# A fused forgetting-attention and gated-FFN kernel: the written issue order and the engines of casts and copies are replaced

## The chip, the cores and the metric

The kernel runs on one core of one Trainium2 chip. The core has five engines with instruction streams of their own: TensorE (PE, matmuls and transposes), VectorE (DVE), ScalarE (ACT), GpSimd (POOL) and SyncE (SP, which here only issues DMA transfers). Each engine works through its own stream in order; semaphores tie the streams together. The metric is the device time of one execution in microseconds (us), as the median of several runs.

## The reference

Two layers are computed. The first is causal attention with a decay, for 8 batches of 8 heads, 576 positions and a head size of 64. The second is a feed-forward layer on its result, 512 to 1024 to 512 wide, with a gate that is a sigmoid of a three-tap convolution along the positions.

```python
scores = scale * np.matmul(q, k.transpose(0, 1, 3, 2))
cum = np.cumsum(np.log(np.clip(f, 0.0001, 1.0)), axis=-1)
scores = np.where(causal, -1e9, scores + cum[:, :, :, None] - cum[:, :, None, :])
attn = softmax(scores)
x = np.matmul(attn, v)                 # (8, 8, 576, 64) -> (8, 576, 512)
h = np.maximum(x @ w_in, 0.0)          # (8, 576, 1024)
conv = conv_w[0] * h[s - 1] + conv_w[1] * h[s] + conv_w[2] * h[s + 1]
out = (h * sigmoid(conv)) @ w_out      # (8, 576, 512)
```

## The kernel before, in words

The work is cut into 16 half-batches (hb) of four heads each for attention, and 8 batches (b) for the feed-forward layer. All of it is written as named tasks. `add` registers a task with its engine, the tasks it comes after, and the buffers it takes and gives back. `Plan.play` then walks through one long list, ORDER, and issues each task in turn. ORDER therefore sets the order of the instructions on every engine and of the transfers on SyncE's queue, and also which of the rotating buffers a task gets. A task name with `@ACT`, `@DVE`, `@POOL` or `@SP` names its engine too, where the task can run on more than one.

The names, for half-batch hb, pair of heads i = 2 hb or 2 hb + 1, batch b, and chunk ff of 128 hidden units:

- Loads on SP: `q{hb}.0` and `q{hb}.1` load the queries and keys of a half-batch by a transposing DMA (line 178); `v{b}.{kb}` loads a block of values of a batch (L207); `wi{j}` and `wo{j}` load quarters of the weights (L496). `rw{hb}` (L200, L201), and from half-batch 8 on `fi{hb}` (L192, L194), put the rows with the decay sums beside the queries and keys; no score of that half-batch can start before them. `s{b}.{a}` stores outputs, `tx14` and `tx15` turn the last attention results by DMA (L416).
- Attention: `cl` clears the odd or even rows of the loaded queries or keys on DVE (L184); for half-batches 0 and 1 it brings in tiles that PE turned (`tp`, L164). `sd`, `so`, `st` are the score matmuls of the diagonal blocks, of the others, and of the tail of 64 positions (L310, with a mask by L318 in half-batches 0 to 7). `ed`, `eo`, `et` are their exponentials on ACT (L351, L368, L330). `md`, `mt` mask on POOL from half-batch 8 on (L354, L333). `va{hb}.0` and `va{hb}.1` cast the values to 16 bits (L215 large, L217 small). `pv` multiplies with the values (L387, L392), `n` divides by the sums (L400, L401), `t` turns the result on PE (L410) and `tx` copies it out of PSUM (L413).
- Feed-forward: `f` first product (L425), `r` relu on ACT (L435), `c` and `d` the two steps of the convolution on DVE (L440, L442), `a` the tanh that makes the sigmoid (L445), `g` the gate on DVE (L449), `o` second product (L456, L460), `e` evacuation of the result (L466, L471). `wic`, `woc` cast the weights (L504).

PSUM is held as four tiles of 128 x 1024, and every PE task but the continuation of a chunk needs a free one. The queries and keys have a ring of four tiles, so the loads of half-batch hb wait for the scores of hb - 4. The values as loaded have two tiles, the cast values four.

SP issues the transfers strictly in their written order, and each engine waits at the head of its stream. So a task that waits holds all that stands behind it on its engine, and a load stands behind all loads written before it.

## Time and profile before

| | us |
|---|---|
| three runs | 249.54, 249.56, 249.83 |
| median | 249.56 |
| profiled execution, from its first to its last instruction (span) | 248.9 |
| median minus span | 0.66 |
| busy in the span: PE, DVE, ACT, POOL | 232.9, 215.9, 211.1, 46.0 |
| granted clock of PE, mean | 0.998 |

Of the profiled execution only the span is told; its time with what lies around it was not noted apart from the runs. The views used below are: the page with the busy time of each engine; the same by stretches of the span; the timeline of an engine, with the start, the length, the line, the operation and what is written from what is read; the groups by line and form, with the busy time of a group, the mean length of one instruction in ns, the idle time before them and what ended it; the waits; and the chain of waits, followed back from the last instruction. A matmul's length in a row holds its pipeline too, so the step from one start to the next is the better price of a matmul.

### The profile page before, as it was taken

To read this page: it belongs to the slowest core of one execution; us is meant where nothing else is said; L and a number is where in the kernel's file an instruction comes from. 1 tells how busy PE (TensorE), PEld (TensorE's weight loads), DVE (VectorE), ACT (ScalarE), POOL (GpSimd) and SP (SyncE) were. 2 spreads that over 40 slices of the span, in tenths; PEclk is the share of its full clock that TensorE was granted. 3 is DMA by queue.
4 is the path that set the end of the run, shared out by engine and by line. 5 is a ranking of instruction groups with operands and counts; after the bars stand their busy time and mean duration, and the time that the engine had idled before them with its cause. 6 is when DMAs were issued, how large, how long until landed. Compare 5 with 4: busy or idle time off the path is not lost.

```text
span 248.9 us, 6646 instructions
## 1 busy us (share of the span) xinstructions
PE 232.9 (94%) x2750; PEld 151.3 (61%) x2750; DVE 215.9 (87%) x328; ACT 211.1 (85%) x286; POOL 46.0 (18%) x76
## 2 busy tenths in 40 slices
PE   0899999879899999999999999999999999999993
PEld 0787785557556856666556765577557756645441
DVE  5654278999999999999999999997999999999961
ACT  2766958999999999979999899998999999767642
POOL 8000411101021501002203070045012502000000
PEclk9999999999999999999999999999999999999999
DMA  7987999999998999999999999899960590223345
GB/s 199 297 157 171 253 226 238 178 276 180 264 201 155 261 173 237 244 250 250 211 271 275 230 188 266 235 230 154 244 188 3 145 320 7 50 47 108 121 153 191
DMA packets 117062, 48.81 MB, mean 196 GB/s; under 512 B 106402, under 2 KB 107618, under 8 KB 117032
## 3 DMA queue, kind: packets, MB, share of 16 engines
q1 hardware_dynamic: 116578, 47.51, 85.3%
q0 software_dynamic: 208, 0.51, 0.7%
q8 instruction: 21, 0.34, 0.6%
q10 hardware_dynamic: 246, 0.37, 0.5%
q14 instruction: 9, 0.07, 0.1%
HBM read 21.11 MB, written 10.17 MB: 126 GB/s over the span
## 4 chain that ended last, share of the span: by engine, by line
PE 68%; DVE 12%; ACT 9%; DMA 6%; issue 3%; ACTq 0%; SPq 0%; DVEq 0%
PE ps L456 18%; PE ps L425 18%; PE ps L310 13%; PE ps L387 6%; PE ps L460 3%; DVE u L440 3%; DMA qk<-in_q_dram 3%; DVE u L442 3%; PE ps L318 2%; DMA u<-in_f_dram 2%; PE ps L410 2%; ACT pp L368 2%; PE ps L392 2%; ACT hg L445 2%; DVE hg L449 2%
## 5 line engine op out<-in xcount | busy, mean ns | idle before, releaser
L425 PE MATMUL ps<-xt,w_in_f 128*128 128x512 f16 (+1 forms) x512 | 68.4, 286 | 1.6 <-DMA xt<-xm 0.6
L368 ACT ACTIVATE pp<-ps 128x1024 f16<-128x1024 f32 x64 | 65.4, 1043 | 4.9 <-PE ps L310 2.6
L310 PE MATMUL ps<-qk 128*128 128x128 bf16 (+2 forms) x576 | 64.4, 241 | 1.8 <-DVE xm L401 0.6
L456 PE MATMUL ps<-w_out_f,hg 128*128 128x512 f16 x256 | 59.2, 379 | 0.0
L442 DVE SCALAR_TENSOR_TENSOR u<-ht,cwt,u 128x576 f32<-128x576 f16 x64 | 53.8, 854 | 1.4
L440 DVE SCALAR_TENSOR_TENSOR u<-ht,cwt 128x576 f32<-128x576 f16 x64 | 53.1, 837 | 2.3 <-ACT ht L435 2.2
L445 ACT ACTIVATE hg<-u,cw 128x576 f16<-128x576 f32 x64 | 48.9, 784 | 5.7 <-DVE u L442 5.7
L425 PEld LDWEIGHTS <-w_in_f 128*128 128x128 f16 x512 | 34.0, 98 | 31.0 <-issue 2.5
L310 PEld LDWEIGHTS <-qk 128*128 128x128 bf16 x576 | 39.6, 98 | 18.9 <-issue 3.8
L449 DVE SCALAR_TENSOR_TENSOR hg<-hg,ht 128x576 f16<-128x576 f16 x64 | 49.8, 800 | 1.0 <-ACT hg L445 0.9
L435 ACT ACTIVATE ht<-ps 128x576 f16<-128x576 f32 x64 | 41.3, 669 | 3.3 <-PE ps L425 3.2
L456 PEld LDWEIGHTS <-hg 128*128 128x128 f16 x256 | 24.0, 98 | 25.9 <-issue 0.2
L354 POOL TENSOR_SCALAR_AFFINE_SELECT pp<-pd 128x1024 f16<-128x1024 f32 x16 | 18.6, 1171 | 48.2 <-ACT pd L351 42.4
L387 PE MATMUL ps<-va,pp 128*128 128x65 f16 x640 | 24.6, 193 | 0.7 <-ACT pp L368 0.5
L401 DVE TENSOR_TENSOR xm<-ps,rc 128x896 f16<-128x896 f32 (+1 forms) x32 | 24.3, 758 | 1.1
L387 PEld LDWEIGHTS <-pp 128*128 128x128 f16 x640 | 22.4, 97 | 3.0 <-ACT pp L368 1.0
L351 ACT ACTIVATE pp<-ps 128x1024 f16<-128x1024 f32 x16 | 16.5, 1038 | 4.7 <-PE ps L315 2.4
L466 ACT COPY ob<-ps 128x1024 f32<-128x1024 f32 (+1 forms) x18 | 15.1, 838 | 3.4 <-PE ps L456 2.5
L351 ACT ACTIVATE pd<-ps 128x1024 f32<-128x1024 f32 x16 | 15.9, 1022 | 1.9 <-PE ps L310 1.9
L318 PE MATMUL ps<-mask,ident 128*128 128x512 bf16 (+1 forms) x40 | 14.8, 369 | 0.3 <-ACT xt L413 0.2
L184 DVE TENSOR_SCALAR qk<-qk,lim 128x2304 uint16<-128x2304 uint16 x12 | 11.2, 933 | 1.1 <-DMA qk<-in_k_dram 0.9
L333 POOL TENSOR_SCALAR_AFFINE_SELECT pt<-p 128x256 f16<-128x256 f32 x8 | 4.8, 596 | 38.6 <-ACT p L330 36.9
(86 smaller groups left out, 193.2 us busy)
## 6 DMA issues: line engine op xcount, KB each, us to landing
vf<-in_v_dram SPq DMA_DIRECT2D x32, 256.0 KB, 4.8
out_dram<-ob SPq DMA_DIRECT2D x14, 512.0 KB, 4.9
qk<-blank SPq DMA_DIRECT2D x8, 540.0 KB, 5.9
ob<-in_moe_w_in_dram SPq DMA_DIRECT2D x4, 512.0 KB, 4.8
ob<-in_moe_w_out_dram SPq DMA_DIRECT2D x4, 512.0 KB, 4.9
vf<-in_v_dram SPq DMA_DIRECT2D x8, 128.0 KB, 5.2
out_dram<-ob SPq DMA_DIRECT2D x4, 256.0 KB, 2.1
out_dram<-ob SPq DMA_DIRECT2D x15, 64.0 KB, 3.2
```

What stands on the lines that cost most here:

```text
L310: nc.tensor.matmul(o, tk[:, h * S + k0:h * S + k0 + 128], tq[:, h * S + q0:h * S + q0 + n], start=first, stop=last and not by_matmul(hb, h))
L351: nc.scalar.activation(o, ps_of(f"sd{i}").rearrange("p (s c) -> p s c", s=2), AF.Exp, scale=SCALE)
L368: nc.scalar.activation(pair(i)[:, s, 512:1536], ps_of(f"so{i}.{s}"), AF.Exp, scale=SCALE)
L387: nc.tensor.matmul(ps[:, c:c + D + 1], block(hb, h, m, n), va[:, h, m, 0:D + 1], start=(m == 0), stop=(m == n))
L401: nc.vector.tensor_tensor(xm[:, CUT * D * u:CUT * D * u + nj * k * D].rearrange("p (j x d) -> p j x d", x=k, d=D), got[:, :, :, 0:D], r.un ...
L425: nc.tensor.matmul(ps[:, t0:t1], w_in_f16[:, cc, 128 * ff:128 * (ff + 1)], xt[:, cc // 2, x:x + t1 - t0], start=(cc == 0), stop=(cc == NCC ...
L435: nc.scalar.activation(ht_of(b, ff)[:, 1:1 + S], ps_of(f"f{b}.{ff}")[:, 0:S], AF.Relu, scale=0.5)
L440: nc.vector.scalar_tensor_tensor(u, ht[:, 0:S], cwt[:, ff, 0:1], ht[:, 1:1 + S], op0=ALU.mult, op1=ALU.add)
L442: nc.vector.scalar_tensor_tensor(u, ht[:, 2:2 + S], cwt[:, ff, 1:2], u, op0=ALU.mult, op1=ALU.add)
L445: nc.scalar.activation(hg_of(b, ff), u_t[slot[f"c{b}.{ff}", "u"]], AF.Tanh, scale=cw[:, ff, 1:2])
L449: nc.vector.scalar_tensor_tensor(hv, hv, 1.0, ht_of(b, ff)[:, 1:1 + S], op0=ALU.add, op1=ALU.mult)
L456: nc.tensor.matmul(ps[:, 512 * (c % 2):512 * (c % 2 + 1)], hg_of(b, ff)[:, 128 * c:128 * (c + 1)], w_out_f16[:, ff, :], **kw)
```

## The change

Only the list ORDER is replaced. It holds the same tasks, each once, and their functions are unchanged; so are the buffers, matmuls and transfers. What moves is the order on all engines and on SP's queue, and the engine of some casts and copies:

| task (lines) | before | after |
|---|---|---|
| large value casts va.0 (L215) | 9 DVE, 3 ACT, 4 POOL | 6 DVE, 1 ACT, 9 POOL |
| small value casts va.1 (L217) | 4 DVE, 6 ACT, 6 POOL | 2 DVE, 6 ACT, 8 POOL |
| copies of turned tiles tx (L413) | 10 DVE, 4 ACT | 9 DVE, 5 ACT |
| large evacuations e (L466) | 1 DVE, 13 ACT | 3 DVE, 11 ACT |
| small evacuations e (L466) | 2 DVE, 5 ACT | 1 DVE, 6 ACT |
| evacuations of the last batch (L471) | 1 DVE, 4 ACT | 5 ACT |
| weight casts wic, woc (L504) | 3 ACT, 5 POOL | 2 ACT, 6 POOL |

The first words of the list, and those at its end from the last product with the values to the first product of batch 7:

```diff
-dca cw ld0 ld0.0.0 tp0.0.0 dcl ld0.1.0 ld0.0.1 tp0.0.1 tp0.1.0 v0.0 ld1 ld0.1.1 ld1.0.1 ld1.0.0 dcs dck q2.1 ki@SP
+ld1 ld0 ld0.0.0 ld0.1.0 ld0.0.1 v0.0 ld0.1.1 ld1.0.1 cw ld1.0.0 dca dcl tp0.0.0 q2.1 tp0.0.1 cl0.0.0@ACT dcs tp0.1.0
...
-pv15.1 r6.7 c6.6 a6.5 o5.2 n15.0 n15.1 tx14 tx15 c6.7 d6.7 a6.7 d6.6 o5.3 g6.3 g6.7 e5.1@ACT f7.0
+pv15.1 n15.0 c6.6 o5.0 r6.7 n15.1 c6.7 o5.1 d6.7 c6.4 s3.1 a6.7 s4.1 s4.2 tx14 g6.7 g6.2 d6.4 a6.3 tx15 r6.5 d6.6 o5.2 c6.5 f7.0
```

SP's queue from the rows of half-batch 6 (the first two rows) to those of half-batch 7 (the last two), before. L178 is a transposing load of queries or keys, L207 a load of values; qk0 to qk3 are the ring, so half-batch 7 is in qk3 and 8 and 9 are in qk0 and qk1:

```order
L200 DMA qk2_87<-image_65 1x2304
L201 DMA qk2_87<-image_65 2x2304
L178 DMA_TRANSPOSE qk3_88<-in_k_dram 128x2304
L207 DMA vf1_90<-in_v_dram 128x8x64
L207 DMA vf1_90<-in_v_dram 64x8x64
L207 DMA vf1_90<-in_v_dram 128x8x64
L178 DMA_TRANSPOSE qk1_86<-in_q_dram 128x2304
L200 DMA qk3_88<-image_65 1x2304
L201 DMA qk3_88<-image_65 2x2304
```

The same piece of SP's queue after the change:

```order
L200 DMA qk2_87<-image_65 1x2304
L201 DMA qk2_87<-image_65 2x2304
L207 DMA vf1_90<-in_v_dram 128x8x64
L178 DMA_TRANSPOSE qk1_86<-in_k_dram 128x2304
L178 DMA_TRANSPOSE qk3_88<-in_q_dram 128x2304
L178 DMA_TRANSPOSE qk1_86<-in_q_dram 128x2304
L207 DMA vf1_90<-in_v_dram 64x8x64
L207 DMA vf1_90<-in_v_dram 128x8x64
L207 DMA vf0_89<-in_v_dram 128x8x64
L200 DMA qk3_88<-image_65 1x2304
L201 DMA qk3_88<-image_65 2x2304
```

Both loads of half-batch 9 (qk1) and a first load of batch 4's values (vf0) now stand ahead of half-batch 7's rows; in the whole queue 52 of these tasks stood ahead of them before and 56 do now, the four more being q9.1, v3.2, v3.3 and v4.0.

POOL's casts ahead of its first masks, before (ob0 to ob2 hold loaded weights, vf0 and vf1 loaded values):

```order
L215 CAST va1_92<-vf0_89 128x4x4x64
L217 CAST va1_92<-vf0_89 64x4x64
L504 CAST w_in_f16_69<-ob0_127 128x2x512
L504 CAST w_in_f16_69<-ob2_129 128x2x512
L504 CAST w_in_f16_69<-ob1_128 128x2x512
L217 CAST va3_94<-vf1_90 64x4x64
L504 CAST w_out_f16_70<-ob2_129 128x1024 x2
```

And after the change:

```order
L504 CAST w_in_f16_69<-ob0_127 128x2x512
L504 CAST w_in_f16_69<-ob1_128 128x2x512
L215 CAST va0_91<-vf0_89 128x4x4x64
L215 CAST va3_94<-vf1_90 128x4x4x64
L504 CAST w_in_f16_69<-ob0_127 128x2x512
L504 CAST w_out_f16_70<-ob1_128 128x1024
L504 CAST w_out_f16_70<-ob0_127 128x1024
L504 CAST w_out_f16_70<-ob2_129 128x1024
L215 CAST va1_92<-vf0_89 128x4x4x64
```

The weights come first on POOL now, and large value casts stand between and behind them.

2 lines of the change are left out of this document (1 added, 1 removed).

## The prediction

> **What bounds the kernel now.** I read the page's busy shares first, then the same by stretches of 10 us, then the timelines of SyncE and TensorE at the places where loads arrive, the chain of waits, and groups by form.
>
> The page's first part:
>
> ```profile
> PE 232.9 (94%) x2750; PEld 151.3 (61%) x2750; DVE 215.9 (87%) x328; ACT 211.1 (85%) x286; POOL 46.0 (18%) x76
> ```
>
> TensorE (PE), VectorE (DVE) and ScalarE (ACT) are all near full over the span. The stretches tell where PE is not full (columns: busy us of PE, PEld, DVE, ACT, POOL with instruction counts, then granted PE clock, DMA share, GB/s):
>
> ```profile
> 40.00:50.00 10.00, 8.94 (x84) 5.25 (x82) 9.69 (x13) 9.76 (x15) 1.96 (x2) 1.00 1.18 198
> 50.00:60.00 10.00, 8.72 (x166) 6.66 (x166) 9.62 (x16) 9.97 (x13) 1.04 (x1) 1.00 1.08 249
> 60.00:70.00 10.00, 8.89 (x84) 5.39 (x82) 9.76 (x15) 10.00 (x14) 1.66 (x1) 1.00 1.05 210
> 70.00:80.00 10.00, 9.96 (x84) 5.42 (x82) 9.93 (x14) 9.82 (x15) 0.00 (x1) 1.00 0.96 196
> 80.00:90.00 10.00, 9.94 (x183) 7.71 (x180) 9.79 (x17) 9.43 (x13) 4.05 (x7) 1.00 1.10 222
> 140.00:150.00 10.00, 9.86 (x157) 7.39 (x154) 9.70 (x15) 9.15 (x14) 5.66 (x5) 1.00 1.12 211
> ```
>
> From 40 to 70 us PE idles 1.06 + 1.28 + 1.11 = 3.45 us, with ACT and DVE both full: those two bound it there. Behind 70 us PE is full and sets the pace. The DMA share is 0.96 to 1.18: the DMA engines are full as well. No instruction is added or removed, so a new order can win little more than those 3.45 us and what PE loses at the end (below). It can lose more than that.
>
> SyncE's timeline (start, length, line, transfer) decides how early attention inputs arrive, since one queue carries all loads in written order:
>
> ```profile
> 15.26 3.44 SPq L178 DMA_TRANSPOSE qk<-in_q_dram  x1
> 19.90 0.32 SPq L200 DMA_DIRECT2D qk<-image  x1
> ...
> 64.02 0.58 SPq L201 DMA_DIRECT2D qk<-image  x1
> ...
> 89.30 0.37 SPq L200 DMA_DIRECT2D qk<-image  x1
> 89.77 0.60 SPq L201 DMA_DIRECT2D qk<-image  x1
> ...
> 92.69 1.20 SPq L207 DMA_DIRECT2D vf<-in_v_dram  x2
> 93.93 3.27 SPq L178 DMA_TRANSPOSE qk<-in_k_dram  x1
> ```
>
> The queue issues nearly back to back; its one early pause is 18.70 to 19.90 us, 1.2 us, ahead of rw1. PE's timeline has the two places where half-batches 4 and 7 are first used:
>
> ```profile
> 66.77 0.38 PE L318 MATMUL ps<-mask,ident 128*128 128x512 bf16 x1
> ...
> 95.85 0.27 PE L318 MATMUL ps<-mask,ident 128*128 128x256 bf16 x1
> ...
> 96.17 1.06 PE L460 MATMUL ps<-w_out_f,hg 128*64 128x256 f16 x16
> ```
>
> The rows of half-batch 4 (rw4) finish issue at 64.60 and PE uses them at 66.77, so they land within 2.17 us. For half-batch 7 the rows finish issue at 90.37, could be used at 92.5, and are used at 95.85: 3.3 us to spare.
>
> **The change part by part.**
>
> *The start, to about 40 us: 0.* ACT, DVE and PE begin with the same tasks; PE's first difference is one score group moved ahead. The loads of w_in move forward on SyncE, ahead of rw1 and the v loads; the 1.2 us pause covers part of it. The first v load may then land up to 3 us later and hold PE by about 1 us, but at half-batch 7 that is absorbed by the wait below. Bounds −0.5 to +1, in the end 0.
>
> *40 to 95 us, compute: up to −2.8, covered by the next term.* I count, in the order, what ACT has to do between f0.3 and f1.7 (before) and between f0.3 and f1.5 (after); both stretches hold the same work of PE to within 0.3 us. After the change ACT has two relus, one tanh and four casts, copies or evacuations of 1024 columns less there; it has two score exponentials, two tail exponentials and two small v casts more. ACT's steps in the chain of waits:
>
> ```profile
> 79.03 1.23 ACT ht L435 x2
> 80.25 0.91 ACT pp L368
> 81.16 0.66 ACT hg L445
> ```
>
> That is 0.62 a relu, 0.91 an exponential, 0.66 a tanh; a copy of 1024 columns is 1.02 (row below), a small one a quarter of the columns, an estimated 0.3. So −1.24 − 0.66 − 4.1 + 1.8 + 1.2 = −3.0, of which I count 2.8 since some of the steps overlap. ACT is a full engine there, so 2.8 of the 3.45 us could come back.
>
> *Half-batch 7 on SyncE: +0.6.* Ahead of rw7 stand all the loads of before plus q9.1 and three v loads (v3.2, v3.3, v4.0). Their price by issue rows: the transpose at 93.93 is 3.3; two v loads take from 92.69 to 93.93, 0.62 each. That makes 5.2. By bytes, 0.59 MB (4 heads of 576 × 64 numbers of 4 bytes) and 3 × 0.26 MB (128 × 512 of them) at 215 GB/s, the mean of the stretches from 40 to 90 us, makes 6.4. I take 6.4, because the DMA engines are full. The pause of 1.2 us is filled now. So rw7 starts at 89.30 + 6.4 − 1.2 = 94.5, finishes 1.07 later, and lands by 97.7. PE reaches its first use (sd14) with st6 and o0.4 done besides. Tasks of their kind stand in the rows above: 95.85 to 96.17, 0.3 us, and the 1.06 us from 96.17, about 1.0 to the next. By the pace of before PE is there at 95.85 + 1.3 = 97.1. Difference +0.6; bounds: 5.2 − 1.2 gives −0.6, 6.4 without the pause gives +1.8. Whatever ACT's relief wins earlier is waited away at this one place, since sd14 stands ahead of everything else on PE.
>
> *From 98 us on: +0.3.* Before t8, t9 and f4.0 some cushions get short: only the nine transposes of t8 stand between pv9.1 and t9, where the second norm of half-batch 9 has to run in between. The nearest price is a short wait that PE has for such a step before (the view of waits: us in total, times, longest):
>
> ```profile
> PE ps L425 <- DVE xt L413: 0.3, 1, 0.3
> ```
>
> One such wait of 0.3 is taken; none, and one at each of the four tight steps (1.2), are the bounds.
>
> *The end: −0.6.* The last turned tiles come by DMA (tx14, tx15). PE's timeline there, before:
>
> ```profile
> 215.69 3.63 PE L456 MATMUL ps<-w_out_f,hg 128*128 128x512 f16 x16
> 219.15 0.65 PE L425 MATMUL ps<-xt,w_in_f 128*128 128x512 f16 x4
> 220.38 2.61 PE L425 MATMUL ps<-xt,w_in_f 128*128 128x512 f16 x20 [0.57 <-DMA xt<-xm]
> ```
>
> Between pv15.1 and f7.0 PE does two chunks of the output product (215.69 to 219.15, 1.73 each) and then waits 0.57 for tx15. After the change three chunks stand there, while DVE puts one more conv (0.81, row below) between the two norms: 1.73 − 0.81 covers 0.57. Bounds −0.6 to 0. Behind the last gate (g7.7) PE had fifteen matmuls of 512 columns and eight pairs of the last chunk to do; nine and seven pairs are left, so DVE may come in later than before by six matmuls before PE waits for it.
>
> *Casts and copies: 0, with a cost if the cover goes.* Rows by form (busy us, mean ns of one):
>
> ```profile
> L215 DVE CAST va<-vf 128x1024 f16<-128x1024 f32 x9 | 7.2, 797 | 5.2 <-DMA vf<-in_v_dram 5.2
> L215 POOL CAST va<-vf 128x1024 f16<-128x1024 f32 x4 | 4.6, 1161 | 33.5 <-DMA vf<-in_v_dram 33.5
> L466 ACT COPY ob<-ps 128x1024 f32<-128x1024 f32 x13 | 13.2, 1017 | 2.5 <-PE ps L456 2.5
> L413 DVE COPY xt<-ps 128x1152 f16<-128x1152 f16 x10 | 7.2, 751 | 1.0 <-PE ps L410 1.0
> ...
> L466 DVE COPY ob<-ps 128x1024 f32<-128x1024 f32 x1 | 1.2, 1217 | 0.0
> ```
>
> DVE gives up three large v casts (2.4 us), a turned copy (0.75) and four small ones (estimated at 0.4 each, half a large one), and takes two large evacuations (2.4): about −2.4 us. POOL takes five large casts (5.8), two small ones and a weight cast (estimated from these rows at 1.2 and 1.3): +8.3 us, on an engine that is 18% busy. But POOL slows DVE. The same DVE operations in a stretch with POOL idle (70 to 80 us) and one with POOL 5.66 us busy (140 to 150):
>
> ```profile
> L440 DVE SCALAR_TENSOR_TENSOR u<-ht,cwt 128x576 f32<-128x576 f16 x4 | 3.2, 810 | 0.0
> L449 DVE SCALAR_TENSOR_TENSOR hg<-hg,ht 128x576 f16<-128x576 f16 x4 | 3.0, 749 | 0.0
> ...
> L449 DVE SCALAR_TENSOR_TENSOR hg<-hg,ht 128x576 f16<-128x576 f16 x5 | 4.2, 879 | 0.0
> L440 DVE SCALAR_TENSOR_TENSOR u<-ht,cwt 128x576 f32<-128x576 f16 x1 | 1.6, 1644 | 0.0
> ```
>
> Excess 0.83 + 5 × 0.13 = 1.5 us for 5.66 of POOL, 0.26 each us. So 8.3 us more of POOL cost DVE 2.2, and its relief of 2.4 is spent. I take 0; bounds −0.5 and +2.2.
>
> [...]
>
> **The sum.** 0 + 0.6 + 0.3 − 0.6 + 0 = +0.3 on the span of 248.9. The median of the runs, 249.56, is 0.66 above the span, taken as unchanged: 249.8.
>
> **The rivals.** *Faster:* the v loads are as cheap as their issue rows and the DMA engines take more at once, so rw7 lands before PE comes and the relief of ACT stays. For it: the 3.45 us of PE idle and ACT's 2.8. Against it: DMA shares of 0.96 to 1.18. It gives between 249.56 − 0.6 − 0.6 = 248.4 (rw7 at its early bound) and 249.56 − 2.8 − 0.6 = 246.2 (no wait at all): 247.3. *Slower by POOL:* between the same f marks POOL had one small and two weight casts and gets three large and four weight casts, most of its 8.3 us, just where DVE is full at 9.62 to 9.76 of 10; if DVE's moved casts are of no use there, the price is 2.2 us. It decides once DVE's norms of half-batches 2 and 3 come later than the rows of half-batch 4, which PE waits for next: 249.8 + 2.2 = 252.0. On the same side, rw7 at its late bound (+1.8 for +0.6) gives 251.0.
>
> **How the numbers follow.** A kernel like this can be told from no change from about 0.2% on, 0.5 us. The wait at half-batch 7, as forecast: chance 0.50, own range 249.0 to 251.0, of which 0.27 lie within 0.2%, 0.20 above and 0.03 below. Faster: 0.25. POOL: 0.25, all slower. Faster 0.28, same 0.27, slower 0.45. The range leaves the outer half of the faster rival and little above POOL's: 247.2 to 252.2.
>
> **What would show it.** Right: rw7 issued at 93.3 to 95.7 us, PE waiting for it just behind, no wait on xt<-xm at the end. Wrong: PE waiting for DVE or POOL at 40 to 70 us, L440 and L449 above 900 ns there; rw7 before 92; or a stall of over 1 us past 100 us, of which no term speaks.

## The result, and the profile after

The new kernel takes 253.85 us (median; 252.69, 253.08, 254.62, 254.91), the kernel before 249.55 on the same chip (249.33 to 249.83). The ratio is 1.0157, 95% interval 1.0127 to 1.0187: slower by 1.6%. The forecast was 249.8 us with a range up to 252.2. Medians here and below are of all runs of a kernel, while the ratios leave out the few that lie over 1.5% above the fastest of their kernel (two of four in e2, one of six in e10 and in b4), and so are not quotients of the medians.

Busy time of the engines over the span of 251.4 us (the profiled execution took 253.08 us):

```profile
PE 231.4 (92%) x2750; PEld 149.8 (60%) x2750; DVE 217.3 (86%) x322; ACT 209.2 (83%) x284; POOL 57.4 (23%) x84
```

POOL is busy 11.4 us longer, and DVE is busier by 1.4 us though it runs six instructions fewer. The stretches of 10 us (columns as in the prediction) tell where PE is not full now:

```profile
40.00:50.00 10.00, 9.29 (x111) 5.79 (x109) 9.12 (x13) 9.48 (x14) 0.00 (x0) 1.00 1.16 202
50.00:60.00 10.00, 7.93 (x110) 5.55 (x108) 9.97 (x15) 9.82 (x14) 2.09 (x2) 1.00 1.03 255
60.00:70.00 10.00, 10.00 (x140) 6.86 (x137) 9.78 (x17) 9.80 (x15) 3.83 (x5) 1.00 1.11 168
130.00:140.00 10.00, 10.00 (x122) 6.36 (x120) 9.77 (x11) 9.08 (x14) 4.96 (x8) 1.00 1.26 218
140.00:150.00 10.00, 8.11 (x131) 5.84 (x130) 9.50 (x16) 7.53 (x11) 1.90 (x3) 1.00 1.19 239
170.00:180.00 10.00, 9.38 (x85) 5.31 (x82) 9.93 (x13) 8.45 (x12) 3.10 (x4) 1.00 0.90 179
```

From 40 to 70 us PE idles 2.78 us instead of 3.45. Behind 80 us, where it was full, it now loses 1.9 us at 140 to 150 and 0.6 at 170 to 180. The place of the 1.9 us, on the timeline (columns: start, length; in brackets the idle time before and what ended it):

```profile
137.16 0.92 POOL L333 TENSOR_SCALAR_AFFINE_SELECT pt<-p 128x256 f16<-128x256 f32 x1
137.73 4.07 DVE L442 SCALAR_TENSOR_TENSOR u<-ht,cwt,u 128x576 f32<-128x576 f16 x2
138.03 0.40 POOL L217 CAST va<-vf 64x256 f16<-64x256 f32 x1
138.37 1.04 POOL L215 CAST va<-vf 128x1024 f16<-128x1024 f32 x1
139.36 1.09 POOL L354 TENSOR_SCALAR_AFFINE_SELECT pp<-pd 128x1024 f16<-128x1024 f32 x1
...
141.99 1.09 DVE L401 TENSOR_TENSOR xm<-ps,rc 128x896 f16<-128x896 f32 x1
143.00 1.22 DVE L466 COPY ob<-ps 128x1024 f32<-128x1024 f32 x1
143.13 0.60 PE L310 MATMUL ps<-qk 128*128 128x64 bf16 x4 [1.27 <-DVE xm L401]
144.26 0.41 PE L387 MATMUL ps<-va,pp 128*128 128x65 f16 x8 [0.53 <-DVE ob L466]
```

The row of DVE at 137.73 is two conv steps, d3.6 and d3.5, that take 0.82 us each where POOL is quiet. Together they take 4.07: d3.6 starts under the mask mt8 and gets through only after POOL has done va11.1, va10.0 and md21 as well, which follow each other without a gap until 140.45. So the norm n8.0 (141.99) is late, and the evacuation e2.1 behind it (143.00), and PE waits for both, 1.27 and 0.53 us.

The same over the whole span: DVE's two conv steps and its gate, before

```profile
L442 DVE SCALAR_TENSOR_TENSOR u<-ht,cwt,u 128x576 f32<-128x576 f16 x64 | 53.8, 854 | 1.4
L440 DVE SCALAR_TENSOR_TENSOR u<-ht,cwt 128x576 f32<-128x576 f16 x64 | 53.1, 837 | 2.3 <-ACT ht L435 2.2
L449 DVE SCALAR_TENSOR_TENSOR hg<-hg,ht 128x576 f16<-128x576 f16 x64 | 49.8, 800 | 1.0 <-ACT hg L445 0.9
```

and after:

```profile
L442 DVE SCALAR_TENSOR_TENSOR u<-ht,cwt,u 128x576 f32<-128x576 f16 x64 | 59.0, 939 | 0.4
L440 DVE SCALAR_TENSOR_TENSOR u<-ht,cwt 128x576 f32<-128x576 f16 x64 | 54.1, 857 | 2.5 <-ACT ht L435 2.3
L449 DVE SCALAR_TENSOR_TENSOR hg<-hg,ht 128x576 f16<-128x576 f16 x64 | 50.1, 801 | 0.3
```

The same 192 instructions take 163.2 us instead of 156.7: 6.5 us more for 11.4 more of POOL.

The rows of half-batch 7, on SyncE and at their first use on PE:

```profile
91.86 0.38 SPq L200 DMA_DIRECT2D qk<-image  x1
92.29 0.60 SPq L201 DMA_DIRECT2D qk<-image  x1
```

```profile
96.19 0.39 PE L318 MATMUL ps<-mask,ident 128*128 128x512 bf16 x1
```

They are issued 2.6 us sooner than forecast, and PE does not wait for them here. At the end no wait on xt<-xm is left, as forecast.

To compare kernels whose orders differ I use PE's lost time: the time up to a task's start, less the price of all tasks that PE did before it (each kind of task at the low fifth of its own steps from start to start). It counts the waits and slow steps of PE in one number. By stretches, in us, from the profiled executions (c0 and c1 are the new kernel again, the others are the experiments below; the tail is from PE's last end to the end of the span):

| profile | to 35 | 35 to 106 | 106 to 135 | 135 to 150 | 150 to 180 | 180 to end | tail |
|---|---|---|---|---|---|---|---|
| before | 12.4 | 6.2 | 0.2 | 0.2 | 0.2 | 1.2 | 4.0 |
| after | 12.6 | 5.0 | 0.2 | 2.4 | 1.3 | 0.6 | 4.9 |
| c0 | 12.6 | 6.6 | 0.2 | 3.9 | 1.3 | 0.5 | 4.9 |
| c1 | 12.2 | 7.1 | 0.1 | 2.4 | 1.3 | 0.6 | 4.8 |
| h1, new to 106, then old | 11.9 | 7.4 | 0.6 | 0.2 | 0.2 | 1.3 | 4.5 |
| e7, two casts later | 12.2 | 6.5 | 0.2 | 0.3 | 1.7 | 0.6 | 4.8 |
| e9, three casts later | 12.2 | 6.2 | 0.2 | 0.3 | 1.1 | 1.4 | 4.8 |
| e8, three casts on ACT | 12.6 | 5.6 | 0.2 | 1.0 | 2.0 | 0.6 | 4.9 |

One profile of before is a thin base for the first two columns: the same task, f1.5, starts at 74.05 us there, and at 73.27 in b1 and 74.58 in h2, which have the same front.

### The profile page after: what moved, and what is told of

The parts are those of the page before. It is cut to its first block, busy times and chain, and to the rows that moved or that the text cites. A ratio compares the mean times of both kernels' runs of the same rounds, so it can differ in the third digit from the quotient of the medians.

```text
span 251.4 us, 6648 instructions
## 1 busy us (share of the span) xinstructions
PE 231.4 (92%) x2750; PEld 149.8 (60%) x2750; DVE 217.3 (86%) x322; ACT 209.2 (83%) x284; POOL 57.4 (23%) x84
## 4 chain that ended last, share of the span: by engine, by line
PE 64%; DVE 20%; ACT 6%; issue 4%; DMA 2%; ACTq 0%; DVEq 0%
PE ps L425 19%; PE ps L456 17%; PE ps L310 11%; DVE u L440 5%; PE ps L387 5%; DVE u L442 5%; DVE hg L449 4%; DVE xm L401 3%; PE ps L460 3%; ACT pp L368 3%; PE ps L164 2%; DMA u<-in_f_dram 2%; PE ps L410 2%; ACT pp L351 2%; PE ps L318 2%
## 5 line engine op out<-in xcount | busy, mean ns | idle before, releaser
L425 PE MATMUL ps<-xt,w_in_f 128*128 128x512 f16 (+1 forms) x512 | 70.2, 286 | 0.8 <-ACT pp L368 0.7
L442 DVE SCALAR_TENSOR_TENSOR u<-ht,cwt,u 128x576 f32<-128x576 f16 x64 | 59.0, 939 | 0.4
L440 DVE SCALAR_TENSOR_TENSOR u<-ht,cwt 128x576 f32<-128x576 f16 x64 | 54.1, 857 | 2.5 <-ACT ht L435 2.3
L445 ACT ACTIVATE hg<-u,cw 128x576 f16<-128x576 f32 x64 | 49.8, 790 | 6.6 <-DVE u L442 6.6
L425 PEld LDWEIGHTS <-w_in_f 128*128 128x128 f16 x512 | 34.1, 98 | 29.4 <-issue 1.7
L354 POOL TENSOR_SCALAR_AFFINE_SELECT pp<-pd 128x1024 f16<-128x1024 f32 x16 | 20.7, 1302 | 72.0 <-ACT pd L351 72.0
L215 POOL CAST va<-vf 128x1024 f16<-128x1024 f32 x9 | 11.3, 1261 | 35.3 <-DMA vf<-in_v_dram 29.1
L351 ACT ACTIVATE pd<-ps 128x1024 f32<-128x1024 f32 x16 | 16.5, 1029 | 1.5 <-PE ps L310 1.4
L466 ACT COPY ob<-ps 128x1024 f32<-128x1024 f32 (+1 forms) x17 | 13.5, 792 | 2.9 <-PE ps L456 1.6
L400 DVE RECIPROCAL rc<-ps 128x14 f32<-128x14 f32 (+1 forms) x32 | 6.6, 208 | 5.4 <-PE ps L387 2.8
```

Of the source, the lines that this page charges most:

```text
L351: nc.scalar.activation(o, ps_of(f"sd{i}").rearrange("p (s c) -> p s c", s=2), AF.Exp, scale=SCALE)
L425: nc.tensor.matmul(ps[:, t0:t1], w_in_f16[:, cc, 128 * ff:128 * (ff + 1)], xt[:, cc // 2, x:x + t1 - t0], start=(cc == 0), stop=(cc == NCC ...
L440: nc.vector.scalar_tensor_tensor(u, ht[:, 0:S], cwt[:, ff, 0:1], ht[:, 1:1 + S], op0=ALU.mult, op1=ALU.add)
L442: nc.vector.scalar_tensor_tensor(u, ht[:, 2:2 + S], cwt[:, ff, 1:2], u, op0=ALU.mult, op1=ALU.add)
L445: nc.scalar.activation(hg_of(b, ff), u_t[slot[f"c{b}.{ff}", "u"]], AF.Tanh, scale=cw[:, ff, 1:2])
```

## The experiments

Theory POOL: casts on POOL hold DVE's instructions off, DVE's norms and evacuations come late, and PE waits. Rivals: the order alone (short cushions, whatever engine casts), SyncE (the rows of half-batch 7, my forecast's own term), and the tail. Each ratio is to the kernel before on the same chip, with its 95% interval.

### Orders and engines exchanged

e1 is the new order with all 36 changed engines as before, e2 with those of the v casts alone, e3 the old order with all the new engines:

```diff
 # e1 (and, for va alone, e2), new order
-wic0@POOL ... va1.0@POOL va0.0@DVE ... va10.0@POOL
+wic0@ACT ... va1.0@DVE va0.0@POOL ... va10.0@POOL
 # e3, old order
-wic0@ACT ... va14.0@DVE ... va15.0@POOL
+wic0@POOL ... va14.0@POOL ... va15.0@DVE
```

> The new order with every cast, copy and evacuation on the engine it had before. Theory POOL (casts on GpSimd hold VectorE off, its norms come late, TensorE waits): POOL's busy time falls from 57.4 to 46 us, the excess of VectorE's conv and gate rows (L440, L442, L449 over 0.81, 0.815 and 0.75 us) falls from 14.2 to about 7 us, the wait at 141 to 143 us goes, and the time is 249.5 to 251.0 us. Rival order (the short cushions of the new order lose the time, whichever engine casts): the waits for L401 at 54 and 141 us stay over 1 us each, 252.5 to 254.5 us. Rival SyncE (the gate at half-batch 7): SyncE's order is kept, so 253 to 255 us. Rival tail (the stores at the end): 0.9 us of the loss stays.

> The new order with only the casts of v (L215, L217) on the engines they had before; weight casts, turned copies and evacuations as in the new kernel, so evacuation e2.1 stays on VectorE. Theory POOL: most of the loss is these casts', POOL about 47 us busy, excess of VectorE's rows about 8 us, 250.0 to 251.5 us. Rival order: 252.5 to 254.5 us. Rival evacuation (the 1.22 us copy e2.1 on VectorE ahead of pv9.1 is to blame): the 0.5 to 0.7 us wait at 144 us stays and so does about 1 us of the loss, 252 to 253.

> The order of before with all 35 moved engines of the new kernel. Theory POOL: the casts cost VectorE there as well, though they meet other instructions: excess of VectorE's rows 10 to 15 us, 251.0 to 254.0 us. Rival order: the order of before has cushions enough, 249.0 to 250.3 us.

Measured: e1 263.33 us, 1.0477 (1.0441 to 1.0512); e2 257.76 (253.96 to 258.08), 1.0173 (1.0076 to 1.0269); e3 261.89, 1.0398 (1.033 to 1.0467). All three lie outside every range given for them. e1 lost its time where no theory had it, on ACT:

```profile
24.54 1.04 ACT L504 CAST w_in_f<-ob 128x1024 f16<-128x1024 f32 x1 [8.41 <-DMA ob<-in_moe_w_in_dram]
```

The new order casts w_in early. On ACT that cast waits 8.4 us for its load with the score exponentials behind it, and PE's longest wait there is 7.6 us. In e2 the large cast va0.0, on POOL again, takes 1.57 us from 30.90, and PE waits 3.3 us for it; in e3 PE waits 2.8 for va14.0 on POOL. Orders and engines fit each other, and an exchange of the one tells little of the other. One reading holds: e2 has va11.1 on DVE again, and its lost time at 135 to 150 is 0.3 us, though the order of PE and the evacuation e2.1 on DVE are the new kernel's.

### The two casts, by engine and by moment

e4 moves only the two casts of the bad place to ACT; e8 moves va13.0 there too. e7 leaves them on POOL and puts them behind the next two masks; e9 also puts va13.0 behind md26. c1 is the new kernel beside e9 on one chip.

```diff
 # e4, e8 (va13.0 in e8 alone)
-va11.1@POOL g3.3 va10.0@POOL ... va13.0@POOL
+va11.1@ACT g3.3 va10.0@ACT ... va13.0@ACT
 # e7, e9 (va13.0 in e9 alone)
-va11.1@POOL g3.3 va10.0@POOL md21 md23 ... ed26 va13.0@POOL ... md26
+g3.3 md21 md23 va11.1@POOL va10.0@POOL ... ed26 ... md26 va13.0@POOL
```

> The new kernel with two casts alone moved from GpSimd to ScalarE: va10.0 (1.04 us at 138.4) and va11.1 (0.40 us at 138.0), the two middle ones of the four GpSimd instructions under which the conv d3.6 took 3.34 us. Theory POOL: d3.6 takes at most 1.7 us, the wait of 1.27 us at 143.1 falls below 0.3, the one at 144.3 below 0.3, and the time falls by 1.3 to 2.0 us to 251.0 to 252.5 us. Rival order: the waits move by less than 0.3 us and the time stays at 252.7 to 254.9 us. If time lost there is given back behind it, the waits go and the time stays.

> The new kernel with the two v casts va11.1 and va10.0 moved behind the mask md23 in GpSimd's order: same engines, same GpSimd work, another moment, so that conv d3.6 and gate g3.7 meet at most two GpSimd instructions in a row there. Theory POOL by the moment: the long row of VectorE (3.3 us of d3.6, 4.4 us of g3.7) falls to at most 1.7 us, the waits of TensorE at 141 to 149 us fall from 2.1 to 3.7 us to under 0.7, and the time falls by 1.3 to 2.5 us against the new kernel, to 0.6 to 1.2% above the kernel before. Theory POOL by the amount (GpSimd's busy time counts, wherever it lies): within 0.5 us of the new kernel, 1.5 to 2.0%.

> The two casts of the earlier run and va13.0 as well on ScalarE instead of GpSimd. va13.0 lies under the convs c4.7 (1.65 us) and d4.7 (1.47) at 172 to 175 us, which hold up the turned copy tx10 that so27.0 waits for (0.6 us on L413 in every run with the new back). Theory POOL: both places clear, c4.7 and d4.7 0.81 us each, the wait on L413 under 0.2, the time 2 to 3 us below the new kernel, 0.4 to 1.0% above the kernel before. Rival: ScalarE, 8.5 of 10 us busy there, is late in their place, and waits for L351 or L368 take back over half: 1.2% or more above.

> The new kernel beside the three that follow, on one chip. All theories: 1.5 to 2.1% above the kernel before.

> The new kernel with three v casts later in GpSimd's order, engines kept: va11.1 and va10.0 behind md23, va13.0 behind md26. Theory POOL by the moment: the waits at 141 to 149 us (2.1 to 3.7) and the one for L413 in front of so27.0 (0.6) both under 0.4 in sum, 2.0 to 3.5 us below the new kernel, 0.4 to 1.0% above the kernel before. Rival order: TensorE finds other short cushions behind (L351, L368), and less than 1.3 us of it stays.

Measured: e4 254.77 us, 1.0142 (1.0094 to 1.0191); e7 252.91, 1.0140 (1.0109 to 1.0170); e8 253.22, 1.0150 (1.0108 to 1.0192). On one chip c1 255.06, 1.0176 (1.0125 to 1.0227), and e9 252.56, 1.0093 (1.0060 to 1.0127): 2.5 us less by the medians, 2.0 by the means, with the same instructions on the same engines. The two intervals just touch. In e9 the two conv steps, and their mask, are

```profile
137.47 1.28 POOL L333 TENSOR_SCALAR_AFFINE_SELECT pt<-p 128x256 f16<-128x256 f32 x2
138.41 1.68 DVE L442 SCALAR_TENSOR_TENSOR u<-ht,cwt,u 128x576 f32<-128x576 f16 x2
139.33 1.73 POOL L354 TENSOR_SCALAR_AFFINE_SELECT pp<-pd 128x1024 f16<-128x1024 f32 x1 [0.57 <-ACT pd L351]
```

1.68 us for the two, 4.08 in c1. PE's lost time at 135 to 150 is 0.3 us in e4, e7 and e9, and 2.4 to 3.9 in the new kernel. POOL's busy time in e9 is 58.7 us, more than in the new kernel, so the moment counts, not the amount. e4, e7 and e8 ran without the new kernel beside them; against its three ratios (1.0157, 1.0196, 1.0176) they are 0.1 to 0.6% better. The waits went as theory POOL has it, but the times of all three stayed above its ranges; e7 too gained less than was expected, though its lost time in all is that of e9.

The second place is so27.0, where the new kernel waits 0.6 us for the turned copy tx10 behind c4.7 and d4.7 (1.65 and 1.47 us), with va13.0 over them. e9 clears it, and gets another wait of 0.46 at 192, behind a gate (g5.5, 1.43 us) that now meets a mask: 0.9 us of lost time between 180 and 200 for the 0.7 saved at 165 to 180. ACT is no free place for the casts: in e8 PE waits for it instead, at 150 and 175 us (in e4 as well, 0.59 us at 154):

```profile
150.40 0.60 PE L310 MATMUL ps<-qk 128*128 128x64 bf16 x4 [0.59 <-ACT pd L351]
...
174.74 1.14 PE L425 MATMUL ps<-xt,w_in_f 128*128 128x512 f16 x8 [0.90 <-ACT pp L368]
```

So by PE's lost time theory POOL holds for the first place, by engine and by moment, and e9 against c1 shows it in the time; for the second place the gain was given back, once to ACT and once to the next collision.

### Halves and the tail

The orders can be cut where both have done nearly the same tasks: near 106 us (h1, h2), and at 232 us, where the sets are equal (h3). c0 is the new kernel beside them.

```diff
 # h1: new order up to va6.0, then the old one; h2: old up to va7.0, then new
 # h3: new up to d7.2, then the old end
-o6.0 a7.2 a7.1 g7.2 c7.3 o6.1 r7.4 r7.6 f7.7 o7.2.0
+f7.4 f7.5 f7.6 f7.7 g7.0 a7.1 g7.1 r7.6 r7.4 s5.2 o6.0
```

> The new kernel once more, beside the three that follow and the kernel before on one chip, since landings and times differ between chips. All theories: 1.0 to 1.9% above the kernel before; waits of 1.2 us or more in front of so23.0 (141 to 143 us) and of 0.5 in front of pv9.1.

> The new order and engines up to the large cast va6.0 (about 106 us), the order and engines of before from there on; where the two orders meet, six tasks are in another place. In the two profiles the new kernel had come to sd14 (96 us) about 0.9 us ahead of the kernel before, measured by the work done. Theory back (the new kernel loses its time behind 106 us, mostly to POOL at 137 to 147): 0.5 to 1.2 us faster than the kernel before. Rival front (the loss of 4 us is earlier and the trace hides it): 2 us or more slower than before. Rival seam (orders and engines only fit as a whole, as the exchange of all engines suggests): slower than both whole kernels.

> The reverse: order and engines of before up to the large cast va7.0 (about 105 us), the new ones from there on. Theory back: the whole loss stays, and the 0.9 us that the new front wins are missing: 3.5 to 5.5 us slower than the kernel before, with the long conv d3.6 (over 3 us) and the wait of 1.2 us in front of so23.0. Rival front: within 1 us of the kernel before. Rival seam: over 6 us slower.

> The new kernel up to f7.3 and d7.2 (about 232 us), where both orders have done exactly the same tasks, and from there the order and engines of before. In the new kernel's profile the end of TensorE's work lies 4.85 us before the end of the span, before the change 4.0. Theory tail: 0.8 to 1.0 us faster than the new kernel. Theory back without the tail: within 0.3 us of it.

Measured: c0 255.07 us, 1.0196 (1.0141 to 1.0252); h1 252.21, 1.0087 (1.0057 to 1.0117); h2 254.04, 1.0163 (1.0113 to 1.0213); h3 253.84, 1.0160 (1.0104 to 1.0216). c0 loses 5.3 us on 249.82, the front alone 2.4 and the back alone 4.2; together somewhat more than the whole, so the seams cost little. Both halves lose, the back more: h2 has d3.5 with 2.97 us under va11.1, va10.0 and md21, and the wait before so23.0. That the front loses was not expected: h1 had been forecast to win 0.5 to 1.2 us. In h1 it waits for the rows of half-batch 7 after all:

```profile
98.12 0.38 PE L310 MATMUL ps<-qk 128*128 128x128 bf16 x4 [0.78 <-DMA qk<-image]
```

The tail is not settled: h3's interval overlaps c0's, its stretch behind PE's end is 4.6 us for 4.9, and it has a new wait of 0.7 before o6.0.

c0's profile shows what the wait at 144 us can bring behind it (columns as above; the granted clock is the third number from the end):

```profile
144.00:145.00 1.00, 0.13 (x2) 0.12 (x2) 1.00 (x2) 1.00 (x2) 0.00 (x0) 1.00 1.07 170
145.00:146.00 1.00, 0.47 (x4) 0.19 (x2) 1.00 (x2) 0.75 (x2) 0.67 (x1) 0.80 1.27 290
146.00:147.00 1.00, 1.00 (x26) 0.90 (x27) 0.47 (x2) 0.53 (x1) 0.76 (x2) 0.50 0.67 140
147.00:148.00 1.00, 1.00 (x20) 0.93 (x15) 0.61 (x2) 0.00 (x0) 0.00 (x0) 0.50 1.01 254
148.00:149.00 1.00, 1.00 (x12) 1.00 (x10) 0.60 (x1) 0.00 (x0) 0.00 (x0) 0.50 0.98 280
149.00:150.00 1.00, 0.92 (x17) 0.64 (x15) 0.82 (x2) 0.56 (x2) 0.00 (x0) 0.99 1.02 345
```

PE's clock is halved for 3.4 us (0.4 of the second row, since 0.80 is 1.00 less half of 0.4, and the next three), and the lost time in this stretch is 3.9 us for the 2.4 of after and c1. More on it in the last section.

### SyncE and half-batch 7

e5 moves the rows of half-batch 7 ahead of the loads of my forecast. e10 (on e9) and b2 (on h1) keep the v loads ahead:

```diff
 # e5
-q9.0 v3.4 ... v3.2 ... v4.0 ... rw7
+rw7 q9.0 v3.4 ... v3.2 ... v4.0
 # e10, b2
-q9.0 v3.4 ... v3.2 ... v4.0 ... rw7
+v3.2 v3.4 rw7 q9.0 v4.0
```

> The new kernel with one task of SyncE moved: rw7, the rows of half-batch 7, now stands ahead of q9.0, v3.4, v3.2 and v4.0 instead of behind them. Theory gate (my forecast's term): TensorE waits for these rows, as it did for 0.78 us in the run with the new front and the old back, so up to 1 us is won: 0.8 to 1.6% above the kernel before. Theory POOL and back: at 96 us the wait is hidden, or what it wins is waited away at 141 us for VectorE; no change against the new kernel: 1.6 to 2.0% above the kernel before, the waits at 141 to 146 us over 2 us in sum.

> The kernel with the three later casts, and on SyncE the loads v3.2, v3.4, then rw7, then q9.0 and v4.0: the rows of half-batch 7 no longer stand behind a transpose of 3.4 us, and the v loads are not later than in the new kernel. Theory gate: rw7 is issued 1.5 to 2.5 us sooner (92 to 93 us instead of 94), the wait at sd14 (0, 0.5 or 1.0 us in the profiles) goes, and 0.4 to 1.0 us are won on the kernel with the three later casts alone. Theory that SyncE has slack here: within 0.3 us of it.

> New front with that order of SyncE's loads, old order and engines from 106 us on. The new front with the old back took 0.87% more than the kernel before, and TensorE waited 0.95 us at sd14. Theory gate: that wait goes, 0.3 to 0.6% above the kernel before. Theory that the front loses elsewhere too (28 to 30 us, 52 to 63 us): over half of the loss stays even without the wait, 0.5 to 0.9%. If ScalarE's relief in the front shows at last: below the kernel before.

Measured: e5 255.53 us, 1.0269 (1.0204 to 1.0334), worse than either theory had it. SyncE stands still:

```profile
82.74 2.83 SPq L178 DMA_TRANSPOSE qk<-in_q_dram  x1
90.46 0.26 SPq L200 DMA_DIRECT2D qk<-image  x1
```

From 85.6 to 90.5 us it waits for DVE's clamp of these queries (cl7.0), which ends only then, and the v loads behind it are late. So DVE waits in its own order, at the cast va7.0:

```profile
98.13 0.69 DVE L215 CAST va<-vf 128x1024 f16<-128x1024 f32 x1 [3.19 <-DMA vf<-in_v_dram]
```

The gate g2.0 behind it gives its buffer back at 102.6, the relu r2.5 has waited 3.0 us for that on ACT and holds a PSUM tile, and PE waits 2.0 us for the tile, up to 103.4. e10: 254.25 us, 1.0129 (1.0075 to 1.0182), no gain on e9's 1.0093; its rows are issued at 93.30 us, right behind the clamp cl7.0, where e9 has 93.41. b2: 251.88, 1.0076 (1.0042 to 1.0111), against 1.0087 for h1: the rows are issued at 92.28 instead of 94.26 and the wait of 0.78 is gone, but most of the front's loss stays. So SyncE's gate can bind, and is worth at most some tenths of a us here; what really holds the rows is the clamp on DVE.

### The front's loads

Last try at the front: the loads of w_in behind the rows and the first v loads, on e9 (e11) and on b2 (b4).

```diff
-wi1 wic1@POOL ... wi0 wic0@POOL ... wi2 ... rw1 ... v0.1 v0.2 v0.3 st0 wi3 rw2 va1.0@POOL ... eo1.1 wic2@ACT
+rw1 ... v0.1 v0.2 v0.3 st0 rw2 va1.0@POOL wi1 wi0 wi2 ... eo1.1 wic1@POOL wic0@POOL ... eo3.0 wic2@ACT wi3
```

> The kernel with the three later casts, and the loads of w_in (wi1, wi0, wi2) on SyncE behind rw1, v0.1 to v0.3 and rw2, wi3 behind eo3.0, with their casts that much later. In the new kernel rw1 is issued at 20.8 us (19.9 before the change) and rw2 at 26.7 (22.9), and TensorE waits 1.2 us for rw1 at 26 us and 0.6 to 1.0 for a cast of v at 30. Theory loads: both waits fall below 0.4, and 0.8 to 2 us are won to the end: 0.1 to 0.6% above the kernel before. Theory gate (as in my forecast: what the front wins is waited away where TensorE next meets SyncE, at half-batch 7 at the latest, since SyncE carries the same loads in all): the lead is there at 35 us and gone at 97, 0.7 to 1.1% above.

> New front with these later loads and with rw7 ahead of q9.0, old order and engines from 106 us on. Theory loads: no later than the kernel before, within 0.2% of it or up to 0.4% faster, since TensorE in the new front is about 1.5 us ahead at 24 us and loses it to these waits. Theory gate: 0.4 to 0.9% above, as without the change of the loads (0.76%).

Measured: e11 256.50 us, 1.0269 (1.0235 to 1.0303); b4 255.06, 1.0190 (1.0155 to 1.0224). The waits at 26 and 30 us did shrink (lost time up to 35 us 11.7 and 11.0, for 12.2 and 12.0 in e9 and b2), and it was lost again ten us on. In e11 DVE, and then PE:

```profile
40.10 0.69 DVE L215 CAST va<-vf 128x1024 f16<-128x1024 f32 x1 [2.78 <-DMA vf<-in_v_dram]
42.35 0.94 DVE L184 TENSOR_SCALAR qk<-qk,lim 128x2304 uint16<-128x2304 uint16 x1 [1.56 <-DMA qk<-in_k_dram]
```

```profile
47.97 4.42 PE L425 MATMUL ps<-xt,w_in_f 128*128 128x512 f16 x17 [4.05 <-ACT pp L368]
```

The v and k loads that now stand behind w_in come late, a cast and a clamp wait for them in DVE's order, the conv steps stand behind both, two tanh on ACT wait for those, and the exponential that frees PE's next PSUM tile stands behind them: PE waits 4.05 us. Behind that wait the clock is at half, still at 52 to 53 us, which neither theory had:

```profile
48.00:49.00 1.00, 1.00 (x5) 0.45 (x5) 1.00 (x2) 1.00 (x2) 0.00 (x0) 0.50 0.86 167
52.00:53.00 1.00, 1.00 (x5) 0.40 (x4) 1.00 (x3) 1.00 (x2) 0.00 (x0) 0.50 1.24 171
```

PE loses another 2.7 us there, and b4, with a wait of 3.96 at the same task, 1.3. So the lead was waited away, as in theory gate, but at 43 us and with interest.

Of what the new front loses, 0.8 to 0.9%, the profiles show one part. DVE's clamp cl4.0 waits for the queries of half-batch 4, the norms of half-batches 2 and 3 stand behind it, and PE waits for them ahead of t2 and t3; in h1:

```profile
60.13 0.88 DVE L184 TENSOR_SCALAR qk<-qk,lim 128x2304 uint16<-128x2304 uint16 x1 [1.35 <-DMA qk<-in_q_dram]
62.34 0.66 PE L410 MATMUL ps<-ident,xm 128*128 128x128 f16 x9 [0.68 <-DVE xm L401]
63.62 0.83 PE L410 MATMUL ps<-ident,xm 128*128 128x128 f16 x9 [0.62 <-DVE xm L401]
```

The two waits of PE add up to 0.85 to 1.37 us in c0, c1, h1, h3, e4, e7 to e10 and b2, to nothing in after and e5, where the clamp does not wait, and to at most 0.1 in the profiles with the old front (before, b1, h2). No run moves this load, so what it is worth in time is not shown, and the rest of the front's loss stays open.

### One task of the end, in the kernel before

```diff
-f7.0 f7.1 r7.0 f7.2 o5.4
+o5.4 f7.0 f7.1 r7.0 f7.2
```

> The kernel before with one task moved: the last chunk o5.4 of the output product (1.0 us of TensorE) ahead of f7.0, where TensorE waits 0.57 us for the turned tile tx15. Theory end (that my forecast priced at 0.6): the wait on xt<-xm goes and 0.3 to 0.7 us are won, 0.1 to 0.3% below the kernel before. Rival: r7.0 comes 0.4 us later, and TensorE waits for the last gates as much longer: within 0.1%.

Measured: 250.15 us, 1.0009 (0.9984 to 1.0033): no change. The wait for tx15 is gone, and PE waits 0.35 for a gate instead:

```profile
239.16 1.06 PE L456 MATMUL ps<-w_out_f,hg 128*128 128x512 f16 x4 [0.35 <-DVE hg L449]
```

No version beat the kernel before.

## Why the prediction was wrong

**The time around the span (0.66).** In every run of these experiments, of before and after alike, the time is 1.66 to 1.79 us above the span. The span of 248.9 so stands for about 250.6 us, 1.0 above the median of before: that profiled execution was probably a long one, and the 0.66 was not the time around it but the difference of two executions. The forecast does not suffer by it, since 248.9 and 0.66 make the median of before again: what was forecast is +0.3 on that median (249.86, given as 249.8), and what came is +4.3. The whole miss of 4.0 us lies in the change.

**Casts and copies (0, bounds −0.5 and +2.2).** This is the step that failed. POOL's extra time was 11.4 us, not 8.3, and a us of it cost DVE 0.57 (6.5 by 11.4), not 0.26. The share of 0.26 was too low for its own stretch already: the view of DVE at 140 to 150 us, before, has one more row that the sum left out,

```profile
L215 DVE CAST va<-vf 128x1024 f16<-128x1024 f32 x1 | 1.6, 1582 | 0.0
```

0.9 us above the 0.69 that such a cast takes at 70 to 80 us; with it the excess is 2.4 us, or 0.42 a us of POOL. And in that stretch two of POOL's masks took 1.59 and 1.54 us (146.78 and 148.33) where those at 164 to 174 us take 1.10, and DVE's cast and the conv behind it (148.84) 1.58 for 0.69 and 1.64 for 0.81, as if each had waited for one of the other engine's. Where four of POOL's follow each other in the new kernel, a conv of DVE's waited out the whole row, 3.34 us for 0.82 in d3.6 (4.07 less 0.73), and up to 4.4 in another execution (g3.7 in c0). A mean share hid this, and so did weighing DVE's loss against DVE's relief as sums. As a sum the relief nearly sufficed, since DVE is busy only 1.4 us longer in all; but it lies elsewhere than the row, and PE waits at the row.

PE's lost time at that one place is 2.4 to 3.9 us in the new kernel and 0.3 with the two casts moved. In time, e9 is 2.0 to 2.5 us below the new kernel of its chip, which had lost 5.0. That gain has three parts that these runs do not separate: this place, the half clock that the wait there can bring (last section), and the second place, of whose 0.7 us nothing was left at 200 us. At this place the price came near the whole of POOL's time: from 137.73 us to the end of the row at 140.45 POOL worked 2.72 us, and d3.6, which got through only when the row's last instruction had ended, lost 2.5 of them.

**The rival "slower by POOL" (252.0, chance 0.25)** had the mechanism and the sign, with the wrong place: I looked for it at half-batches 2 and 3, where POOL's order changed most, and it came at half-batches 8 and 9. PE does wait for norms at 54 to 63 us too, but not by POOL: the wait of 1.4 us at 55 is for n2.0, and in the 15 us up to 53 POOL did nothing, and those for t2 and t3 come from a load, as shown above. That 252.0 lies near the result is in part luck, since the front's loss of 2.4 us is in the result as well. Of the signs that I had set for being wrong, the stall of over 1 us past 100 us came, and, in the first profile alone, rw7 ahead of 92 us; PE's wait for DVE at 55 came without the rows above 900 ns that were to go with it (L440 has 890 at 40 to 70 us).

**From 98 us on (+0.3, bounds 0 to 1.2).** I named the neighbourhood, pv9.1, t8 and t9, but another wait: that of t9 for the second norm of half-batch 9, which did not come. PE waits just ahead of it, at so23.0 and pv9.1, for the tiles of n8.0 and e2.1, and with that norm late by 2.5 us it loses 2.1; the bound of 1.2 was too low. In e9, with the same order of PE, ACT and DVE, the place costs 0.3: the cushions were enough, what they had to cover was not as forecast.

**Half-batch 7 on SyncE (+0.6, rows issued at 94.5, range 93.3 to 95.7).** In the first profile of after the rows came at 91.86 and nothing waited. In the later profiles with this front and this order of loads they came at 93.4 to 94.7 (c0, c1, h1, h3, e7, e8, e9), as forecast, and at 97.0 in e4; PE waited 0.8 in h1, 0.5 in e7, 0.3 in e4 and not in the others. So the time was right for most executions and the wait mostly too high; the step decided nothing. Its working left out the clamp on DVE, which e5 shows to be the real gate.

**Start (0) and ACT's relief (up to −2.8, covered).** Lost time up to 35 us is 12.2 to 12.6 for 12.4: right, as far as one profile of before can tell. Of the relief 1.2 us shows in the first profile (35 to 106 us, 5.0 for 6.2) and nothing in c0 and c1: covered, as said, but by waits ahead of 65 us, those for t2 and t3 above all, and not by half-batch 7.

**The end (−0.6).** Right: no wait on xt<-xm, lost time behind 180 us 0.5 to 0.6 for 1.2. But the time from PE's end to the span's end grew by 0.8 us, of which no term spoke; the four stores of the last batch go out between 244.6 and 247.1 us in one row, spread over 3.1 us before. h3 did not settle it.

## What to carry to other kernels

Price work on POOL by the place, not by a mean share: look for spots where several POOL instructions become ready together (masks of two half-batches and a cast whose load has long landed), and ask which DVE instruction starts under the first of them and who waits for it. A cast that may run any time can go behind the masks in POOL's order rather than on the next engine, which may be as full; here that cleared the first place without a new wait, while at the second the next mask met a gate and cost as much. And a price taken from a stretch must take in every row of that stretch that is longer than elsewhere.

## What was not expected of the hardware

**Behind some waits of PE the granted clock was at half.** It is at 0.50 for 3.4 us or twice that: in c0 at 145.6 to 149.0 us, after a wait of 1.48 us and during one of 0.53; in e3 at 219.8 to 223.2 after 2.8; in e2 at 32.5 to 35.9 after 3.3; in e1 at 22.6 to 29.4, after 3.7 us of a wait of 7.6; in e11 from 46.7 us to 53 at least, late in a wait of 4.05; in b4, with a wait of 3.96, somewhere in 44.2 to 50.6 us, where the page has a clock of 0.7; and in e5, where the wait is only

```profile
103.40 1.17 PE L387 MATMUL ps<-va,pp 128*128 128x65 f16 x32 [2.04 <-ACT ht L435]
```

and the clock behind it

```profile
104.00:105.00 1.00, 1.00 (x23) 0.78 (x20) 1.00 (x3) 1.00 (x2) 0.00 (x0) 0.84 1.29 303
105.00:106.00 1.00, 0.96 (x4) 0.25 (x2) 1.00 (x2) 1.00 (x3) 0.00 (x0) 0.50 1.08 422
...
107.00:108.00 1.00, 1.00 (x4) 0.32 (x3) 0.96 (x2) 1.00 (x2) 0.00 (x0) 0.50 0.98 237
```

Much the same waits, 1.27 and 0.53 us, leave the clock at 1.00 in after and c1. The clock records of the traces show one pattern. In before they begin at 15.76 us and hold full clock for 232.11 us, in after they begin at 13.71 and hold it for 235.52: 68 and 69 times 3.413. The stretches at half read from the 1 us windows of c0, e2, e3 and e5 are 3.4 us long each, that of e1 6.8. Cut into steps of 3.413 us from the first record, no step of before has PE idle for more than 0.90 us and none of after for more than 1.50 (27.36 to 30.77 us), but for the last one of each, at PE's end, with 2.98 and 2.70 us idle, and behind that one the clock is at half. Counted back from the fall of the clock, the step ahead of it has PE idle for 1.61 us in c0, 2.04 in e5, 2.78 in e3, 3.3 in e2 and 3.4 in e1, while e3 has one (182.25 to 185.67) with 1.5 to 1.7 and no fall. In c0 that step, 142.19 to 145.60, holds the whole first wait; in after a step ends at 143.41, between the two waits, and the two steps have 1.27 and 0.59 us idle. Read so, what came behind much the same waits hung on where the steps fell. That is a reading of these seven traces; what sets the clock is not shown.

Of the 14 runs of the new kernel, seven with a mean clock of at most 0.993 have a mean of 255.5 us, the seven above it 253.4; 3.4 us at half clock would account for 1.7 of these 2.1, an estimate (half of 3.4). The eleven runs of e7 and e9, without the wait, all have 0.995 or more; of the eight of h2 and h3, which have it, one is lower (0.991).

**POOL's row can hold DVE.** Of the 192 convs and gates, the 156 of before and the 155 of after that meet no instruction of POOL are at most 0.01 us over 0.81 (convs) or 0.75 (gates). A conv of after that starts with a mask (164.86, 1.10 us) takes 1.70 us, 0.89 more. A row of POOL's without a gap need not add more: in after and c1 the gate g3.7 gets in behind three of the row of seven, with 1.63 us, 0.88 more, and the mask mt8 behind it takes 0.92 us where mt9 takes 0.41. But it can: d3.6 then takes 3.34 us under the four that are left, and in c0 g3.7 waits out all seven, with 4.38. The gate in c1, and the same in c0:

```profile
137.84 1.63 DVE L449 SCALAR_TENSOR_TENSOR hg<-hg,ht 128x576 f16<-128x576 f16 x1
```

```profile
137.71 4.38 DVE L449 SCALAR_TENSOR_TENSOR hg<-hg,ht 128x576 f16<-128x576 f16 x1
```

What decides whether DVE gets in is not shown.
